# Sink-window attention with a two-layer MLP on one core: start-up order, three engine moves and the last output step

## The chip, the cores and the metric

One core of a Trainium2 chip runs the kernel. Its engines work side by side and meet at semaphores: TensorE (PE, with the weight loads shown apart as PEld), VectorE (DVE), ScalarE (ACT), GpSimd (POOL), and SyncE (SP), whose queue issues nearly all DMAs. Each engine works through its own list in order. The metric is device time in microseconds (us), as the median of three runs.

## The reference

Batch 4, 8 heads, 768 positions, head size 64, float32. Query i sees keys of a window, `0 <= i - k < window` (128 here), and the first `n_sink` keys (4 here):

```python
keep = is_sink | in_window
scores = np.where(keep, scale * q @ k.T, -1e9)
a = exp(scores - max); a = a / (sum(a) + 1e-9)
x = (a @ v)                       # heads side by side: 3072 tokens x 512
h = x @ w_in                      # 512 x 2048
g = np.maximum(0.01 * h, h)
out = g @ w_out                   # 2048 x 512
```

`n_sink` and `window` come as data, so the masks are computed on the chip.

## The kernel before, in words

The work is cut into 8 units (a batch's first or second 384 tokens), named u. A unit has an attention part, four head pairs, and an MLP part, 16 steps over the hidden dimension (fc). A unit's MLP needs x of its four pairs.

**Start.** `body` makes `ident` (for transposes on PE) and calls `build_masks`. That loads the two limits by DMA and writes masks m0, m1, m2 (for the first, second and later query tiles), and also what only units 2 to 7 use: `tri`, `low`, `upp` and the packed masks `pm`. GpSimd writes rel, key, low, upp, and copies m1 to m2 (line 89) after DVE has made m1. Only behind that copy, in `fast_path`, GpSimd zeroes `wz` (line 211), the operand of WARM = 16 small bf16 matmuls that open PE's list (line 216), and the sink buffers `sk` (line 220).

**Attention of units 0 and 1** ("native", both heads of a pair at once). For each query tile j: the scores on PE (line 240), max with the mask on DVE (line 252), exp on ACT (line 254), a copy of the four sink columns to `sk` on GpSimd (line 388). Then, some tile steps later (LAGT, LAGG, LAGV), PE transposes the weights (line 279) and ACT copies them to `pt` (line 283); `gather` transposes the sink weights and the reciprocal sums (lines 305, 309), which ACT and DVE copy out (lines 313, 316, 317); `values` multiplies with v (line 326) and with the sink values sv (line 333). DVE scales the result (line 339), ACT rounds it to xh (line 340) and GpSimd makes the remainder xl (line 341). The sink values arrive by DMA as svr; ACT rounds them to sv (line 194), GpSimd subtracts (line 195).

**Weights.** Each of 16 w_in and 16 w_out tiles arrives as 64-bit words and is decoded by three DVE instructions (lines 141, 143, 145), rounded by ACT (line 149), and its remainder made by GpSimd (line 150). The first is told to stand behind an attention instruction on DVE (`tc.issue_after`). Three fc are loaded during unit 0's attention, the others in unit 0's MLP.

**MLP.** Step fc puts 12 matmuls h (line 465: four x tiles, three terms each) on PE; ACT, DVE, ACT, GpSimd make g, gh and gl from it (lines 472 to 475, 2.7 us in a row); then PE runs the o matmuls of the step before it: gh with both halves of w_out for each of three token tiles (line 487), then gl for the three (line 492). With fc = 15 the three tiles are copied out by DVE (line 503; the very last tile in halves, ACT at line 498 and DVE at line 500) and written by SP.

**Order.** PE's list is written out by hand: `attention_stream` and `mlp_stream` are generators. 32 + LEAD0 steps of attention go first (32 are unit 0's), then attention steps are taken between MLP steps at due times that rise from LEAD0 to LEAD = 12 steps ahead. The lists of the other engines and of SP are made by the framework's planner from the program's order and its own time model. Pools of buffers set when a tile may be written: tag io has three buffers (svr, decoded weights, outputs), tag raw three, tag qksp (the q and k of a pair, qkn) two.

Of the kernel before, what the change touches and what calls it, by code (L numbers as in the profile page):

```python
# [12 lines left out]
I8 = mybir.dt.int8  # L13
# [27 lines left out]
LEAD = 12  # L41
LEAD0 = 5
LAGT = 2
# [5 lines left out]
PRED = 3  # L49
WARM = 16  # L50
W_LO = 1.125 * 2.0 ** -15
# [4 lines left out]
def build_masks(nc, cpool, tpool, lims):  # L56
# [31 lines left out]
    nc.vector.tensor_scalar(out=m1, in0=m1, scalar1=-1.0, scalar2=MASKED, op0=ALU.add, op1=ALU.mult)  # L88
    nc.gpsimd.tensor_copy(out=m2, in_=m1)
    nc.vector.tensor_scalar(out=m2[:, snk], in0=key[:, 0:NSK], scalar1=ns, scalar2=-1.0, op0=ALU.is_lt,  # L90
                            op1=ALU.add)
    nc.vector.tensor_scalar(out=m2[:, snk], in0=m2[:, snk], scalar1=MASKED, scalar2=None, op0=ALU.mult)
    tri = cpool.tile([P, P], I8, name="tri")
    low = cpool.tile([P, P], F32, name="low")
    upp = cpool.tile([P, P], F32, name="upp")
    nc.vector.tensor_scalar(out=tri, in0=rel[:, P:], scalar1=0.0, scalar2=None, op0=ALU.is_lt)
    nc.gpsimd.memset(low, 1.0)
    nc.gpsimd.affine_select(out=upp, in_=low, pattern=[[1, P]], base=0, channel_multiplier=-1,
                            compare_op=ALU.is_ge, fill=0.0)
    nc.gpsimd.affine_select(out=low, in_=low, pattern=[[-1, P]], base=-1, channel_multiplier=1,  # L100
                            compare_op=ALU.is_ge, fill=0.0)
    pm = [m0]
    for i, m in enumerate((m1, m2)):
# [3 lines left out]
        pm.append(pk)  # L107
    return lim, (m0, m1, m2), pm, tri, low, upp


@with_exitstack
def fast_path(ctx, tc, cpool, qp, qk, vu, vs, wq, out, ident, lim, masks, pmasks, tri, low, upp, negm, wmin,
              wmax):
    nc = tc.nc
# [13 lines left out]
    raws, vraws, svs = {}, {}, {}  # L128
    sks = []

# [59 lines left out]
    def load_sinks(u, pair):  # L190
        raw = iopool.tile([SKR, TU], F32, tag="io", name=f"svr{u}_{pair}", bufs=3)
        nc.sync.dma_start(out=raw, in_=vs[u // 2, pair])
        sv = apool.tile([SKR, TU], F32R, tag="sv", name=f"sv{u}_{pair}")
        nc.scalar.copy(out=sv, in_=raw)
        (nc.gpsimd if native(u) else nc.vector).tensor_tensor(out=sv[D:96, :], in0=raw[D:96, :],
                                                              in1=sv[D:96, :].bitcast(F32), op=ALU.subtract)
        svs[u, pair] = sv
# [11 lines left out]

    wz = wpool.tile([P, 2 * P], mybir.dt.bfloat16, name="wz")  # L210
    nc.gpsimd.memset(wz, 0.0)
    warm = bank("h", "warm")
# [72 lines left out]
    def turn_packed(u, pair, o, w, state):  # L285
# [12 lines left out]
        n = T - 1 + half  # L298
        for t, mask in enumerate((low, upp)):
            nc.vector.tensor_tensor(out=dst[:, t], in0=src,  # L300
                                    in1=mask.rearrange("p (o q) -> p o q", o=1).broadcast_to([P, n, P]), op=ALU.mult)
# [18 lines left out]
    def values(u, pair, state):  # L320
# [16 lines left out]
        if native(u):  # L337
            xf = state["r"]
            nc.vector.tensor_tensor(out=xf, in0=acc[:, 0:TU], in1=xf, op=ALU.mult)
            nc.scalar.copy(out=xh, in_=xf)  # L340
            nc.gpsimd.tensor_tensor(out=xl, in0=xf, in1=xh.bitcast(F32), op=ALU.subtract)  # L341
        else:
            nc.scalar.copy(out=xh, in_=acc[:, 0:TU])
            nc.vector.tensor_tensor(out=xl, in0=acc[:, 0:TU], in1=xh.bitcast(F32), op=ALU.subtract)
# [7 lines left out]
    def attend(u, pair, pend):  # L352
# [3 lines left out]
        def later(lag, f):  # L356
            pend.append((count[0] + lag, f))
# [19 lines left out]
        if native(u):  # L377
            state["sm"] = apool.tile([P, T, 2], F32, tag="sm", name=f"sm{u}_{pair}")
            sp = raws.pop((u, pair))
            for j in range(T):  # L380
# [10 lines left out]
                if j == 0:  # L391
                    fetch(0)
                    load_sinks(u, pair)
                count[0] += 1
                if j == T - 1:
# [3 lines left out]
        else:  # L399
            for o in range(2):  # L400
# [8 lines left out]
                for j in range(T):  # L409
                    ps, = scores(u, pair, j, (o,), sp)  # L410
                    if KSL[u % 2][j][1] == W3:
                        nc.vector.copy_predicated(out=ps[:, W1:W3], mask=tri, data=ps[:, 0:P])
                        src = ps[:, P:W3]
                    else:
                        src = ps[:, 0:W1]
                    soft(u, h, j, w[:, j], src, pmasks[min(T * (u % 2) + j, 2)], sm[:, j:j + 1])
                    count[0] += 1
# [9 lines left out]
                    yield  # L427
        later(LAGG, lambda: gather(u, pair, state))
        later(LAGV, lambda: values(u, pair, state))

# [18 lines left out]
    def mlp_stream():  # L449
        po = {}  # L450
        prev = None
        for step in range(NU * NFC + 1):
# [26 lines left out]
            if prev is not None:  # L479
                v, f, gh, gl = prev  # L480
                if f == 0:
                    po = [bank(f"o{t}", f"o{v}_{t}") for t in range(T)]
                wh, wl = wts["o", f]
                for t in range(T):
                    tsl = slice(t * P, (t + 1) * P)
                    for c, w in enumerate((wh, wl)):
                        nc.tensor.matmul(po[t], lhsT=gh[:, tsl], rhs=w, start=f == 0 and c == 0, stop=False)  # L487
                    if t < T - 1:
                        yield v
                for t in range(T):  # L490
                    tsl = slice(t * P, (t + 1) * P)
                    nc.tensor.matmul(po[t], lhsT=gl[:, tsl], rhs=wh, start=False, stop=f == NFC - 1)  # L492
                    if f == NFC - 1:
                        last = v == NU - 1 and t == T - 1
                        ob = iopool.tile([P, 512], F32, tag="raw" if last else "io", name=f"ob{v}_{t}", bufs=3)
                        r0 = (v * T + t) * P
                        if last:
                            nc.scalar.copy(out=ob[:, 0:256], in_=po[t][:, 0:256])
                            nc.scalar.dma_start(out=out[r0:r0 + P, 0:256], in_=ob[:, 0:256])
                            nc.vector.tensor_copy(out=ob[:, 256:], in_=po[t][:, 256:])  # L500
                            nc.sync.dma_start(out=out[r0:r0 + P, 256:], in_=ob[:, 256:])
                        else:
                            nc.vector.tensor_copy(out=ob, in_=po[t])
                            nc.sync.dma_start(out=out[r0:r0 + P, :], in_=ob)
                yield v
# [164 lines left out]
def body(tc, qp0, qp1, qk0, qk1, vu0, vu1, vs, wq, qT, kT, v, lims, w_in, w_out, out):  # L670
# [3 lines left out]
    wq = wq.bitcast(I32)  # L674
    with tc.tile_pool(name="cpool", bufs=1) as cpool:
        ident = cpool.tile([P, P], F32, name="ident")
        make_identity(nc, ident)
# [3 lines left out]
        with tc.tile_pool(name="tpool", bufs=1) as tpool:  # L681
            lim, masks, pmasks, tri, low, upp = build_masks(nc, cpool, tpool, lims)
        flag = fast_path(tc, cpool, (qp0, qp1), (qk0, qk1), (vu0, vu1), vs, wq, out, ident, lim, masks,
                         pmasks, tri, low, upp, negm, wmin, wmax)
        bad = nc.values_load(flag[0:1, 0:1], min_val=0, max_val=1)
# [49 lines left out]
```

## Time and profile before

| what | us |
|---|---|
| median of 3 runs | 722.77 (722.31 to 724.15) |
| the profiled execution: its own time | 722.46 |
| its span, first to last instruction | 720.7 |
| busy: PE, DVE, POOL, ACT | 689.8, 430.1, 371.4, 346.9 |

A row of the timeline gives the start, the duration, the engine, line and operation, the tile written and those read, and in brackets the idle time of the engine before it with what ended it. A row of windows gives busy time by engine in a stretch, then PE's granted clock as a share of 2.4 GHz, the DMA share and rate.

### The profile page before, as it was taken

To read this page: it belongs to the slowest core of one execution; us is meant where nothing else is said; L and a number is where in the kernel's file an instruction comes from. 1 tells how busy PE (TensorE), PEld (TensorE's weight loads), DVE (VectorE), ACT (ScalarE), POOL (GpSimd) and SP (SyncE) were. 2 spreads that over 40 slices of the span, in tenths; PEclk is the share of its full clock that TensorE was granted. 3 is DMA by queue.
4 is the path that set the end of the run, shared out by engine and by line. 5 is a ranking of instruction groups with operands and counts; after the bars stand their busy time and mean duration, and the time that the engine had idled before them with its cause. 6 is when DMAs were issued, how large, how long until landed. Compare 5 with 4: busy or idle time off the path is not lost.

```text
span 720.7 us, 11518 instructions
## 1 busy us (share of the span) xinstructions
PE 689.8 (96%) x3917; PEld 594.5 (82%) x3917; DVE 430.1 (60%) x1190; ACT 346.9 (48%) x938; POOL 371.4 (52%) x424
## 2 busy tenths in 40 slices
PE   6879989999999999999999999999999999999995
PEld 3448778888888888887898888888888888799894
DVE  5866989765557576665667676675566755411111
ACT  4765575554444555445555454545554444222221
POOL 4666677644354665655665565556556443122220
PEclk9899999999999999999999999999999999999998
DMA  6656566341222533253332534334342400001001
GB/s 215 219 168 194 180 205 216 123 147 38 67 70 88 170 107 120 80 157 131 121 108 82 181 106 126 114 99 158 108 135 80 132 16 1 1 0 45 1 1 49
DMA packets 30307, 78.51 MB, mean 109 GB/s; under 512 B 3488, under 2 KB 9888, under 8 KB 30240
## 3 DMA queue, kind: packets, MB, share of 16 engines
q1 hardware_dynamic: 30096, 77.56, 33.8%
q8 instruction: 33, 0.54, 0.3%
q14 instruction: 34, 0.28, 0.1%
q10 hardware_dynamic: 144, 0.13, 0.1%
HBM read 71.39 MB, written 6.29 MB: 108 GB/s over the span
## 4 chain that ended last, share of the span: by engine, by line
PE 83%; DVE 6%; ACT 3%; DMA 3%; issue 2%; POOL 2%; DVEq 0%; POOLq 0%; ACTq 0%; SPq 0%
PE h L465 33%; PE o L487 23%; PE o L492 11%; PE acc L326 5%; PE s L245 4%; DMA svr<-in_vs 2%; PE t L289 2%; ACT pk L254 2%; PE acc L333 2%; PE s L240 1%; PE t L279 1%; POOL zero L160 1%; DVE g L473 1%; PE warm L216 1%; DVE pk L421 1%
## 5 line engine op out<-in xcount | busy, mean ns | idle before, releaser
L475 POOL TENSOR_TENSOR gl<-g,gh 128x384 fp32r<-128x384 f32 x127 | 138.9, 1094 | 200.4 <-ACT gh L474 197.4
L465 PE MATMUL h<-xh,wih 128*128 128x384 f32 x512 | 180.3, 352 | 2.0 <-DVE g L473 2.0
L465 PE MATMUL h<-xl,wih 128*128 128x384 f32 x512 | 172.4, 337 | 0.7 <-POOL xl L341 0.7
L465 PE MATMUL h<-xh,wil 128*128 128x384 f32 x512 | 172.6, 337 | 0.0
L487 PE MATMUL o<-woh,gh 128*128 128x512 f32 x384 | 155.8, 406 | 2.9 <-ACT gh L474 2.9
L487 PE MATMUL o<-wol,gh 128*128 128x512 f32 x384 | 151.7, 395 | 0.0
L473 DVE TENSOR_TENSOR g<-h,g 128x384 f32<-128x384 f32 x128 | 71.3, 557 | 111.9 <-ACT g L472 110.4
L474 ACT CAST gh<-g 128x384 fp32r<-128x384 f32 x128 | 65.5, 512 | 93.7 <-DVE g L473 92.5
L492 PE MATMUL o<-woh,gl 128*128 128x512 f32 x384 | 109.8, 394 | 0.0
L465 PEld LDWEIGHTS h<-xh,wih 128*128 128x128 f32 x512 | 96.5, 188 | 10.7 <-DVE g L473 2.4
L254 ACT ACTIVATE pk<-pk,negm 128x132 f32<-128x132 f32 (+1 forms) x192 | 81.4, 424 | 44.6 <-DVE negm L252 43.4
L465 PEld LDWEIGHTS h<-xl,wih 128*128 128x128 f32 x512 | 96.7, 189 | 5.8 <-POOL xl L341 1.1
L472 ACT ACTIVATE g<-h 128x384 f32<-128x384 f32 x128 | 62.4, 487 | 74.8 <-PE h L465 74.2
L465 PEld LDWEIGHTS h<-xh,wil 128*128 128x128 f32 x512 | 96.2, 188 | 0.0
L492 PEld LDWEIGHTS o<-woh,gl 128*128 128x128 f32 x384 | 72.2, 188 | 17.1
L204 POOL TENSOR_TENSOR qksp<-qkraw,qksp 64x396 fp32r<-64x396 f32 (+1 forms) x48 | 56.6, 1178 | 57.6 <-issue 51.7
L487 PEld LDWEIGHTS o<-woh,gh 128*128 128x128 f32 x384 | 72.7, 189 | 11.7 <-ACT gh L474 4.2
L487 PEld LDWEIGHTS o<-wol,gh 128*128 128x128 f32 x384 | 72.6, 189 | 7.0
L245 PEld LDWEIGHTS s<-qksp 128*128 128x128 f32 x288 | 53.2, 188 | 6.4
L203 ACT CAST qksp<-qkraw 128x780 fp32r<-128x780 f32 (+1 forms) x48 | 42.9, 894 | 28.4 <-PE s L245 26.8
L245 PE MATMUL s<-qksp 128*128 128x260 f32 (+1 forms) x288 | 56.1, 276 | 0.0
L160 POOL TENSOR_SCALAR zero<-mag 128x512 f32<-128x512 f32 x32 | 48.0, 1500 | 15.7 <-ACT mag L159 9.1
(109 smaller groups left out, 911.7 us busy)
## 6 DMA issues: line engine op xcount, KB each, us to landing
craw<-in_wq SPq DMA_DIRECT2D x32, 512.0 KB, 3.9
qkraw<-in_qk SPq DMA_DIRECT2D x24, 454.0 KB, 3.2
qkraw<-in_qk SPq DMA_DIRECT2D x24, 390.0 KB, 3.0
wiraw<-in_wq SPq DMA_DIRECT2D x16, 512.0 KB, 3.9
woraw<-in_wq SPq DMA_DIRECT2D x16, 512.0 KB, 3.6
svr<-in_vs SPq DMA_DIRECT2D x32, 192.0 KB, 2.8
out<-ob SPq DMA_DIRECT2D x23, 256.0 KB, 2.6
v<-in_vu SPq DMA_DIRECT2D x16, 256.0 KB, 3.0
```

Of the source, the lines that this page charges most:

```text
L160: nc.gpsimd.tensor_scalar(out=zero, in0=mag, scalar1=0.0, scalar2=None, op0=ALU.is_equal)
L203: nc.scalar.copy(out=sp[:, 0:TU + n], in_=raw[:, 0:TU + n])
L204: nc.gpsimd.tensor_tensor(out=sp[D:P, TU:TU + n], in0=raw[D:P, TU:TU + n], in1=sp[D:P, TU:TU + n].bitcast(F32), op=ALU.subtract)
L245: nc.tensor.matmul(pss[0][:, 0:kn], lhsT=sp[:, off + j * P:off + (j + 1) * P], rhs=sp[:, TU + k0:TU + k0 + kn], start=c == 0, stop=c == 1)
L254: nc.scalar.activation(out=w, in_=w, func=AF.Exp, scale=-1.0, bias=neg, accum_out=sm)
L465: nc.tensor.matmul(ph[:, 0:TU], lhsT=w[:, cs], rhs=x, start=cc == 0 and c == 0, stop=cc == NCC - 1 and c == 2)
L472: nc.scalar.mul(g, ph[:, 0:TU], 0.01)
L473: anchor[0] = nc.vector.tensor_tensor(out=g, in0=ph[:, 0:TU], in1=g, op=ALU.max)
L474: nc.scalar.copy(out=gh, in_=g)
L475: (nc.vector if step == NU * NFC - 1 else nc.gpsimd).tensor_tensor(out=gl, in0=g, in1=gh.bitcast(F32), op=ALU.subtract)
L487: nc.tensor.matmul(po[t], lhsT=gh[:, tsl], rhs=w, start=f == 0 and c == 0, stop=False)
L492: nc.tensor.matmul(po[t], lhsT=gl[:, tsl], rhs=wh, start=False, stop=f == NFC - 1)
```

## The change

- The zeros `wz` move to `body`, ahead of `ident`: they are GpSimd's first work of the kernel. WARM goes from 16 to 17.
- `build_masks` keeps m0, m1 and m2; m2's copy from m1 becomes two copies without the sink columns. `late_masks` writes low, upp, tri and pm, and is called in unit 0's third pair, behind its sink load. tri, a DVE compare before, becomes a GpSimd select and a copy; the select uses a buffer of tag io.
- In unit 0 the rounding of svr to sv goes from ACT to GpSimd, and so does that of x to xh for pairs 0 to 2.
- The last pair of unit 0 gathers and sums after LAGT = 2 tile steps in place of 3 and 4, and LEAD0 goes from 5 to 3, so PE's list has two steps of unit 1's attention fewer ahead of the first h.
- The o matmuls are one list. Up to fc = 14 their order is as before, with the places at which attention steps may come in moved to behind each third. With fc = 15 they run tile by tile (gh, gh, gl), and each tile is copied out as its third matmul is placed.

```diff
-LEAD0 = 5
+LEAD0 = 3
-WARM = 16
+WARM = 17
...
-    nc.gpsimd.tensor_copy(out=m2, in_=m1)
+    nc.gpsimd.tensor_copy(out=m2[:, prv], in_=m1[:, prv])
+    nc.gpsimd.tensor_copy(out=m2[:, cur], in_=m1[:, cur])
...
+def late_masks(nc, cpool, tpool, masks):
+    m0, m1, m2 = masks
...
-    nc.vector.tensor_scalar(out=tri, in0=rel[:, P:], scalar1=0.0, scalar2=None, op0=ALU.is_lt)
     nc.gpsimd.memset(low, 1.0)
     nc.gpsimd.affine_select(out=upp, in_=low, pattern=[[1, P]], base=0, channel_multiplier=-1,
                             compare_op=ALU.is_ge, fill=0.0)
+    sel = tpool.tile([P, P], F32, tag="io", name="sel", bufs=3)
+    nc.gpsimd.affine_select(out=sel, in_=low, pattern=[[1, P]], base=-1, channel_multiplier=-1,
+                            compare_op=ALU.is_ge, fill=0.0)
     nc.gpsimd.affine_select(out=low, in_=low, pattern=[[-1, P]], base=-1, channel_multiplier=1,
                             compare_op=ALU.is_ge, fill=0.0)
+    nc.gpsimd.tensor_copy(out=tri, in_=sel)
     pm = [m0]
     for i, m in enumerate((m1, m2)):
         nc.gpsimd.tensor_copy(out=pk[:, 0:NSK], in_=m[:, snk])
         nc.vector.tensor_tensor(out=pk[:, NSK:], in0=m[:, prv], in1=m[:, cur], op=ALU.max)
...
-        nc.scalar.copy(out=sv, in_=raw)
+        (nc.scalar.copy if u else nc.gpsimd.tensor_copy)(out=sv, in_=raw)
...
-    wz = wpool.tile([P, 2 * P], mybir.dt.bfloat16, name="wz")
-    nc.gpsimd.memset(wz, 0.0)
...
-            nc.scalar.copy(out=xh, in_=xf)
+            (nc.gpsimd.tensor_copy if u == 0 and pair < NPAIR - 1 else nc.scalar.copy)(out=xh, in_=xf)
...
                     load_sinks(u, pair)
+                    if u == 0 and pair == 2:
+                        late.append(late_masks(nc, cpool, iopool, masks))
...
-        later(LAGG, lambda: gather(u, pair, state))
-        later(LAGV, lambda: values(u, pair, state))
+        last = u == 0 and pair == NPAIR - 1
+        later(LAGT if last else LAGG, lambda: gather(u, pair, state))
+        later(LAGT if last else LAGV, lambda: values(u, pair, state))
...
-                for t in range(T):
+                order = [(t, c) for t in range(T) for c in range(2)] + [(t, 2) for t in range(T)]
+                if f == NFC - 1:
+                    order.sort()
+                for i, (t, c) in enumerate(order):
                     tsl = slice(t * P, (t + 1) * P)
-                    for c, w in enumerate((wh, wl)):
-                        nc.tensor.matmul(po[t], lhsT=gh[:, tsl], rhs=w, start=f == 0 and c == 0, stop=False)
-                    if t < T - 1:
+                    nc.tensor.matmul(po[t], lhsT=(gl if c == 2 else gh)[:, tsl], rhs=wl if c == 1 else wh,
+                                     start=f == 0 and c == 0, stop=f == NFC - 1 and c == 2)
+                    if i in (2, 5):
                         yield v
-                for t in range(T):
-                    tsl = slice(t * P, (t + 1) * P)
-                    nc.tensor.matmul(po[t], lhsT=gl[:, tsl], rhs=wh, start=False, stop=f == NFC - 1)
-                    if f == NFC - 1:
+                    if f < NFC - 1 or c < 2:
+                        continue
...
+        wz = cpool.tile([P, 2 * P], mybir.dt.bfloat16, name="wz")
+        nc.gpsimd.memset(wz, 0.0)
         ident = cpool.tile([P, P], F32, name="ident")
```

## Rows read from the trace of the kernel before

**Rows 1.** The page's first part: busy time, share of the span, instructions.
```profile
PE 689.8 (96%) x3917; PEld 594.5 (82%) x3917; DVE 430.1 (60%) x1190; ACT 346.9 (48%) x938; POOL 371.4 (52%) x424
```
**Rows 2.** Windows: the first unit's attention, two parts of it, its MLP.
```profile
10.54:46.80 36.26, 29.28 (x194) 17.62 (x193) 26.29 (x96) 28.28 (x93) 20.65 (x47) 0.91 0.58 195
20.20:27.90 7.70, 7.43 (x33) 4.35 (x33) 6.16 (x19) 4.84 (x15) 4.52 (x8) 0.56 0.54 178
27.90:37.70 9.80, 7.39 (x57) 4.33 (x55) 8.05 (x26) 8.74 (x28) 7.30 (x15) 1.00 0.77 260
46.80:135.00 88.20, 83.54 (x480) 68.80 (x478) 74.23 (x162) 54.88 (x133) 66.16 (x77) 0.98 0.61 192
```
**Rows 3.** Timeline of the start: a mask, the zeros, warm-up, scores, first weight decode.
```profile
5.42 0.22 DVE L84 TENSOR_SCALAR m<-m 128x132 f32<-128x132 f32 x1
...
6.76 0.31 POOL L211 MEMSET wz<- 128x256 bf16 x1 [0.20 <-DVE m L90]
...
7.13 3.48 PE L216 MATMUL warm<-wz 128*128 128x256 bf16 x16 [7.13 <-POOL wz L211]
...
10.54 1.80 PE L240 MATMUL s<-qkn 64*128 64x132 f32 x12
11.06 0.30 DVE L252 CUSTOM_DVE_ANT_0 pk<-s,m 128x132 f32<-128x132 f32 x1 [3.97 <-PE s L240]
...
13.82 0.69 DVE L141 TENSOR_SCALAR di<-wiraw 128x512 int32<-128x512 int32 x1
```
**Rows 4.** SP's queue: the first load of q and k, the first weight load.
```profile
1.25 0.42 SPq L174 DMA_DIRECT2D qkn<-in_qp  x1
...
4.10 0.43 SPq L136 DMA_DIRECT2D wiraw<-in_wq  x1
```
**Rows 5.** From issue to landing, us: that load of qkn, then that wiraw.
```profile
DMA to landing us min/median/max: 3.8/3.8/3.8
...
DMA to landing us min/median/max: 5.6/5.6/5.6
```
**Rows 6.** Groups by line up to 46.8 us: casts, copies and selects that move.
```profile
L194 ACT CAST sv<-svr 128x384 fp32r<-128x384 f32 x6 | 3.1, 511 | 8.9 <-DMA svr<-in_vs 8.5 <-PE acc L333 0.4
...
L266 POOL COPY rb<-sm 128x384 f32<-128x384 f32 x5 | 2.5, 505 | 1.4 <-DVE sm L264 1.4
...
L98 POOL TENSOR_SCALAR_AFFINE_SELECT upp<-low 128x128 f32<-128x128 f32 x1 | 0.3, 288 | 0.0
```
**Rows 7.** Timeline of ACT: a sink rounding that waited for its DMA.
```profile
40.54 0.51 ACT L194 CAST sv<-svr 128x384 fp32r<-128x384 f32 x1 [2.03 <-DMA svr<-in_vs]
```
**Rows 8.** Timeline: one DVE instruction twice, the second beside a GpSimd one.
```profile
14.57 0.17 DVE L263 TENSOR_SCALAR sm<-sm 128x6 f32<-128x6 f32 x1
...
29.81 1.27 POOL L150 TENSOR_TENSOR wol<-wo,woh 128x512 fp32r<-128x512 f32 x1 [0.33 <-PE t L279]
...
30.10 1.00 DVE L263 TENSOR_SCALAR sm<-sm 128x6 f32<-128x6 f32 x1
```
**Rows 9.** Timeline of PE: the same four transposes in two stretches.
```profile
23.95 1.11 PE L279 MATMUL t<-ident,pk 128*128 128x128 f32 x4
...
31.57 0.66 PE L279 MATMUL t<-ident,pk 128*128 128x128 f32 x4
```
**Rows 10.** Timeline of the end: the last gl, o, copies and output DMA.
```profile
710.39 0.56 DVE L475 TENSOR_TENSOR gl<-g,gh 128x384 fp32r<-128x384 f32 x1 [0.58 <-ACT gh L474]
...
710.56 0.40 PE L487 MATMUL o<-woh,gh 128*128 128x512 f32 x1
...
711.96 0.86 PE L492 MATMUL o<-woh,gl 128*128 128x512 f32 x3
712.40 1.29 DVE L503 COPY ob<-o 128x512 f32<-128x512 f32 x2 [1.45 <-PE o L492]
...
713.60 0.41 DVE L500 COPY ob<-o 128x256 f32<-128x256 f32 x1
...
714.28 0.41 SPq L501 DMA_DIRECT2D out<-ob  x1
```

More of the change, by code (lines that the diff above doesn't have):

```diff
@@ L92, in build_masks @@
     nc.vector.tensor_scalar(out=m2[:, snk], in0=m2[:, snk], scalar1=MASKED, scalar2=None, op0=ALU.mult)
-    tri = cpool.tile([P, P], I8, name="tri")
+    return lim, (m0, m1, m2)
+def late_masks(nc, cpool, tpool, masks):
+    m0, m1, m2 = masks
+    prv, snk, cur = slice(0, P), slice(P, W1), slice(W1, W3)
     low = cpool.tile([P, P], F32, name="low")
     upp = cpool.tile([P, P], F32, name="upp")
-    nc.vector.tensor_scalar(out=tri, in0=rel[:, P:], scalar1=0.0, scalar2=None, op0=ALU.is_lt)
+    tri = cpool.tile([P, P], I8, name="tri")
     nc.gpsimd.memset(low, 1.0)
@@ L107, in build_masks, with fast_path @@
         pm.append(pk)
-    return lim, (m0, m1, m2), pm, tri, low, upp
+    return pm, tri, low, upp
 @with_exitstack
-def fast_path(ctx, tc, cpool, qp, qk, vu, vs, wq, out, ident, lim, masks, pmasks, tri, low, upp, negm, wmin,
-              wmax):
+def fast_path(ctx, tc, cpool, qp, qk, vu, vs, wq, out, ident, lim, masks, wz, negm, wmin, wmax):
     nc = tc.nc
@@ L128, in fast_path @@
     raws, vraws, svs = {}, {}, {}
-    sks = []
+    sks, late = [], []
     def load_weights(fc):
@@ L298, in turn_packed @@
         n = T - 1 + half
-        for t, mask in enumerate((low, upp)):
+        for t, mask in enumerate(late[0][2:]):
             nc.vector.tensor_tensor(out=dst[:, t], in0=src,
@@ L411, in attend @@
                     if KSL[u % 2][j][1] == W3:
-                        nc.vector.copy_predicated(out=ps[:, W1:W3], mask=tri, data=ps[:, 0:P])
+                        nc.vector.copy_predicated(out=ps[:, W1:W3], mask=late[0][1], data=ps[:, 0:P])
                         src = ps[:, P:W3]
@@ L415, in attend @@
                         src = ps[:, 0:W1]
-                    soft(u, h, j, w[:, j], src, pmasks[min(T * (u % 2) + j, 2)], sm[:, j:j + 1])
+                    soft(u, h, j, w[:, j], src, late[0][0][min(T * (u % 2) + j, 2)], sm[:, j:j + 1])
                     count[0] += 1
@@ L489, in mlp_stream @@
                         yield v
-                for t in range(T):
-                    tsl = slice(t * P, (t + 1) * P)
-                    nc.tensor.matmul(po[t], lhsT=gl[:, tsl], rhs=wh, start=False, stop=f == NFC - 1)
-                    if f == NFC - 1:
[L494 to L504, printed above, removed]
+                    if f < NFC - 1 or c < 2:
+                        continue
@@ new lines, in mlp_stream @@
+                    last = v == NU - 1 and t == T - 1
+                    ob = iopool.tile([P, 512], F32, tag="raw" if last else "io", name=f"ob{v}_{t}", bufs=3)
+                    r0 = (v * T + t) * P
+                    if last:
+                        nc.scalar.copy(out=ob[:, 0:256], in_=po[t][:, 0:256])
+                        nc.scalar.dma_start(out=out[r0:r0 + P, 0:256], in_=ob[:, 0:256])
+                        nc.vector.tensor_copy(out=ob[:, 256:], in_=po[t][:, 256:])
+                        nc.sync.dma_start(out=out[r0:r0 + P, 256:], in_=ob[:, 256:])
+                    else:
+                        nc.vector.tensor_copy(out=ob, in_=po[t])
+                        nc.sync.dma_start(out=out[r0:r0 + P, :], in_=ob)
@@ L681, in body @@
         with tc.tile_pool(name="tpool", bufs=1) as tpool:
-            lim, masks, pmasks, tri, low, upp = build_masks(nc, cpool, tpool, lims)
+            lim, masks = build_masks(nc, cpool, tpool, lims)
         flag = fast_path(tc, cpool, (qp0, qp1), (qk0, qk1), (vu0, vu1), vs, wq, out, ident, lim, masks,
-                         pmasks, tri, low, upp, negm, wmin, wmax)
+                         wz, negm, wmin, wmax)
         bad = nc.values_load(flag[0:1, 0:1], min_val=0, max_val=1)
```

## The prediction
> **What bounds the kernel now.** I read the page's first part, then windows, then the timeline of the stretches in which PE isn't full. PE is busy 96% of the span [rows 1], so a gain can come from two places: PE's idle time, and PE's time at a low clock. The windows show where that is [rows 2]. Unit 0's attention, from the first score at 10.54 to the first h at 46.8, is 36.3 us with PE busy 29.3; its MLP, to 135, is 88.2 us with PE busy 83.5. What comes later is PE's own work, and no engine move of the change reaches it. In the attention stretch no engine is full: ACT is busy 28.3 of 36.3, DVE 26.3, GpSimd 20.7. It is a chain of short steps through four engines, in which whoever is late holds PE, whose list is in fixed order.
>
> Ahead of it stand 10.54 us without a score. The timeline tells why [rows 3]: the zeros are written at 6.76, behind the last mask on DVE, so the 16 warm-up matmuls run from 7.13 to 10.61 and the first score follows at once. The scores' data came much earlier: the load issued at 1.25 [rows 4] landed 3.8 us later [rows 5], at 5.05. The mask of the first tile was done at 5.64 [rows 3]. So the zeros alone kept PE's list shut.
>
> **The change, part by part.**
>
> *Zeros first, 17 warm-ups.* GpSimd can write the zeros at the place of its first memset, before 1.2 us. I put PE's start there. At 3.48 / 16 = 0.217 us each [rows 3], 17 take 3.7 us, so they end at about 4.9, where the data lands at 5.05. First score near 5.1, that is 5.4 us earlier. The first mask step needs m0, done at 5.64, so it can stand near 5.7 in place of 11.06: also 5.4 less. The first weight decode limits this. It stands at 13.82 [rows 3], after seven mask steps and before the rest of pair 1's, and DVE can't pass it. Its DMA was issued at 4.10 [rows 4] and landed 5.6 us later [rows 5], at 9.7. These loads don't move: they wait for no engine. If DVE's list keeps its order, the decode starts at 9.7, so the stream behind it moves up by 13.82 − 9.7 = 4.1. If the planner puts mask steps ahead of it, up to 5.4. If the later masks (m2's two copies are on GpSimd now and follow m1) are put ahead of the first mask step, that one stands near 7 and the gain at that place is 4, much the same. Lower end 3, for a first mask step at 7 with its chain then late at the decode as well. I take **4.1**: it is the end that a row fixes.
>
> *Late masks.* They take from the start one GpSimd memset and two selects, which had waited for nothing there, and add to the middle of unit 0 five GpSimd instructions of 128x128 (0.29 each by the select's row [rows 6], so 1.4 us) with two tiny copies, and on DVE two max instructions, which leave the start. tri's select holds an io buffer for a moment; SP's next sink load or the next weight may wait for it, and with the planner free to move them I price it with the next item.
>
> *sv and xh on GpSimd.* A rounding of 128x384 costs ACT 0.511; GpSimd's copy of the same shape, from another source, costs 0.505 [rows 6]. Seven go over in unit 0: ACT loses 3.6 us, GpSimd gains 3.5. In the middle (27.9 to 37.7) ACT is busy 8.74 of 9.80 and GpSimd 7.30 [rows 2]. Four of the seven can fall there: ACT goes to 6.7. GpSimd gets 2.0, and 1.4 of masks: 10.7 for 9.8. So the chain is freed at one engine and filled at the other. Best end: what ACT sheds is all on the path, +2.0. Worst end: the 3.4 us stand ahead of a sink copy or a reciprocal that PE waits for, −3.4. I take **0**, between the two. ACT's wait of 2.03 at 40.54 [rows 7] stays: that sink load is unit 1's first, and unit 1's rounding stays on ACT. In the sum it goes nowhere; if it goes away as the lists shift, +2.0 more.
>
> *LAGT for the last pair, LEAD0 3.* PE's list has gather and values of the last pair one step after the other, and h two attention steps earlier. PE's work is the same, so only idle time can go. PE is idle 36.3 − 29.3 = 7.0 us in the attention stretch and 88.2 − 83.5 = 4.7 in the MLP [rows 2]; the two steps that move touch only the end of the one and the start of the other. Against a gain: values now follows gather with no score between them, and x of the last pair is made in a chain that h waits for; and unit 0's MLP takes 41 attention steps in place of 39, while DVE is busy there 74.2 of 88.2 [rows 2]. Bounds +1.5 and −1.5. I take **+0.4**, near zero, since the chain from gather to xl is as long as before.
>
> *The last o step.* At the end PE runs six o matmuls from 710.56 and three from 711.96 (0.233 each), then DVE copies two whole tiles from 712.40 and half of the last at 713.60, and SP issues that half's DMA at 714.28 [rows 10]. Tile by tile, the first tile's gl is wanted at 710.56 + 2 × 0.233 = 711.02; DVE has written it at 710.95, so no wait. The first tile is complete near 711.4, the second near 712.1, each copied (0.65) before the next; the last is complete at 712.82 as before, and its half is copied from 712.9 to 713.3. The DMA goes out near 713.35 in place of 714.28, behind less traffic: **+1.0** (bounds 0.6 and 1.8). At the seven other unit ends nine o matmuls (2.1 us at 0.233) and twelve h matmuls lie between a step's h and its o, so gl is there in time; 0. The places at which attention may come in move by a matmul or two: 0, and with it ±0.5.
>
> *Sum.* 4.1 + 0 + 0.4 + 1.0 = 5.5 us. Against the profiled execution's own 722.46 (1.8 more than its span, which I leave as it is) that is 717.0. The median is 0.3 above it, so **717.3**.
>
> **A cost that the sum leaves out, by row and by rule.** DVE's small step on the sums took 0.17 us once and 1.00 while GpSimd subtracted [rows 8]. The Trainium skill, "SBUF — State Buffer", section "SBUF: two separate sides", says that DVE and GpSimd share a pair of ports under a lock, held for a whole instruction, so that one blocks fully. The rows agree: the long one ends when the subtraction does. By that rule each of the seven moved roundings could hold a DVE step, up to 3.5 us in all, a sum of 2.0 in place of 5.5.
>
> **Rivals.**
>
> *A, more than the sum.* The window 20.2 to 27.9 has a mean granted clock of 0.56 (1.00 is 2.4 GHz), with PE busy 7.43 of 7.70 [rows 2]. At 2.4 GHz that work is 7.43 × 0.56 = 4.2, so 3.3 us go if the stretch doesn't come back. With ACT's 2.0 from [rows 7] the gain is up to 10.8. For it: ACT is the engine with the least to spare in the attention stretch, and it sheds work. Against: four of its seven roundings may come only after that window. Time 711.5 to 715.
>
> *B, GpSimd becomes the bound.* The 3.4 us of the middle are all late, ahead of the copies that gather needs, or the lock above takes as much from DVE: 5.5 − 3.4 = 2.1, so **720.6**. For it: GpSimd's 10.7 of 9.8. Against: sink roundings and masks can be done early or in gaps; over the whole stretch GpSimd has 15 us free.
>
> *C, the change doesn't do what it says.* The planner places the first mask step behind work that waits, or a DMA that the shifted stream asks for lands late, and what the start gives is idle time again before the first h. Only the tail is left: about **721.8**. Against: the rows show data and mask at 5.05 and 5.64.
>
> *D, slower.* One mechanism: the clock. The warm-up now runs while the loads are still under way, and the first scores then wait for masks; if PE has the low level through unit 0's attention, its work there is longer. The same four transposes take 1.11 at the low level and 0.66 at the high one [rows 9], ratio 1.68. PE's busy time outside the low window is 29.3 − 7.4 = 21.9; × 0.68 = 14.9 more, less what idle time takes up (36.3 − 29.3 = 7.0): 7.9, so **725.2**. It decides once over 5.5 of these 7.9 us come, so two thirds of the attention at the low level. Against: in the kernel before 16 warm-ups were enough; in the window behind the low one the clock is 1.00 under the same kind of work [rows 2].
>
> **How the numbers follow.** The sum (715 to 719.6): 0.56. A: 0.17. B (719.6 to 721): 0.14. C: 0.06. D: 0.07. The likeliest is 717.3. The range 713.0 to 721.0 takes in most of A and all of B; under 0.2 is left out, on A's far end, C and D. A measurement of this kernel tells a change from none at about 0.3%, 2.2 us: below 720.6 is faster. All of the first two, and about 0.10 of B: 0.83. C and the rest of B: 0.10. D: 0.07.
>
> **What would show it.** Right: warm-up from near 1.2 to 4.9, first score near 5.1, first mask step between 5.7 and 7, first decode near 9.7 with DVE idle ahead of it, first h near 41, the last output DMA issued 0.9 us sooner after the last matmul. GpSimd's busy time up to the first h should rise by some 5 us and ACT's fall by 3.6. Wrong: a first h later than 44 (B, C or D, told apart by who PE waits for and by the granted clock), or PE idle in unit 0's MLP well over 4.7 us, which would mean that what the start gave is taken back there.

## The result, and the profile after

The changed kernel takes 715.99 us (715.04 to 717.52, 4 runs) against 722.54 (721.5 to 724.15, 4 runs): ratio 0.9909 [0.9884, 0.9935], so 6.5 us sooner. The profiled execution of it is the slowest of its four, 717.52; its span is 715.8, against 720.7, so the traces explain 4.9 of the 6.5.

The first part of the page (compare [rows 1]): PE does the same work. Of the moves one sees ACT fall and GpSimd rise.
```profile
PE 689.6 (96%) x3918; PEld 594.5 (83%) x3918; DVE 423.8 (59%) x1189; ACT 344.9 (48%) x931; POOL 377.0 (53%) x434
```

The timeline of the start (compare [rows 3]):
```profile
0.80 0.31 POOL L688 MEMSET wz<- 128x256 bf16 x1 [0.29 <-POOLq L738]
...
1.17 3.81 PE L223 MATMUL warm<-wz 128*128 128x256 bf16 x17 [1.17 <-POOL wz L688]
...
5.13 0.93 PE L247 MATMUL s<-qkn 64*128 64x132 f32 x8
...
5.71 0.22 DVE L84 TENSOR_SCALAR m<-m 128x132 f32<-128x132 f32 x1
...
6.38 0.29 DVE L259 CUSTOM_DVE_ANT_0 pk<-s,m 128x132 f32<-128x132 f32 x1
...
9.74 0.69 DVE L150 TENSOR_SCALAR di<-wiraw 128x512 int32<-128x512 int32 x1 [0.53 <-DMA wiraw<-in_wq]
```
The first score stands 5.41 us sooner (5.13 for 10.54), the first mask step 4.68, the first decode 4.08 (9.74 for 13.82), and DVE is idle for 0.53 ahead of it, for the weight's DMA. Up to here the trace is what the prediction wrote down. But the first h starts at 45.05. The mark set for it was near 41, and 4.1 sooner alone would be 42.7.

Windows of the kernel after (compare [rows 2]): first score to first h, unit 0's MLP up to the first h of unit 1's, and from there to the first h of the very last step ("the last h" below). The prediction's window of unit 0's MLP ended at 135.00; unit 1's first h is at 142.73, and PE's idle time up to there is the same 4.7 us.
```profile
5.13:45.05 39.92, 29.44 (x184) 17.89 (x185) 26.82 (x101) 25.40 (x83) 27.19 (x62) 0.87 0.64 217
45.05:139.14 94.09, 91.12 (x527) 75.04 (x526) 79.90 (x181) 60.14 (x148) 70.30 (x84) 1.00 0.60 191
139.14:701.79 562.65, 558.67 (x3165) 493.93 (x3164) 312.69 (x895) 256.72 (x696) 276.76 (x278) 1.00 0.28 89
```
The last two of these stretches in the kernel before:
```profile
46.79:142.73 95.94, 91.28 (x521) 75.65 (x519) 79.27 (x176) 59.32 (x145) 70.12 (x82) 0.98 0.58 181
142.73:706.39 563.66, 559.41 (x3165) 493.75 (x3164) 318.39 (x894) 255.66 (x695) 274.44 (x278) 1.00 0.28 89
```
This is the account of the 4.9 us. Start: 5.41 gained. Unit 0's attention: 39.92 in place of 36.25, 3.67 given back; PE is busy about as long (29.44, 29.27), so it is idle for 10.5 us where it was for 7.0. Unit 0's MLP: 1.85 gained. The rest up to the last h: 1.01. From the last h to the end: 14.28 became 14.03, 0.25. In this execution most of what the start gave is gone again by the first h, and stretches from which the sum took little or nothing gained.

### The profile page after: what moved, and what is told of

Read it like the earlier page. It is cut to its first block, busy times and chain, and to the rows that moved or that the text cites. A ratio compares the mean times of both kernels' runs of the same rounds, so it can differ in the third digit from the quotient of the medians.

```text
span 715.8 us, 11514 instructions
## 1 busy us (share of the span) xinstructions
PE 689.6 (96%) x3918; PEld 594.5 (83%) x3918; DVE 423.8 (59%) x1189; ACT 344.9 (48%) x931; POOL 377.0 (53%) x434
## 4 chain that ended last, share of the span: by engine, by line
PE 87%; DMA 4%; DVE 3%; ACT 2%; POOL 2%; issue 1%; SPq 1%; ACTq 0%; POOLq 0%; DVEq 0%
PE h L475 35%; PE o L499 35%; PE acc L333 5%; PE s L252 4%; PE t L296 2%; DMA svr<-in_vs 2%; PE acc L340 2%; PE s L247 1%; PE t L286 1%; DMA craw<-in_wq 1%; DMA wiraw<-in_wq 1%; PE sk L312 0%; DMA out<-ob 0%; DVE wi L154 0%; DVE di L150 0%
## 5 line engine op out<-in xcount | busy, mean ns | idle before, releaser
L485 POOL TENSOR_TENSOR gl<-g,gh 128x384 fp32r<-128x384 f32 x127 | 141.1, 1111 | 204.9 <-ACT gh L484 204.7
L499 PE MATMUL o<-woh,gh 128*128 128x512 f32 x384 | 151.5, 395 | 2.5 <-ACT gh L484 2.5
L499 PE MATMUL o<-woh,gl 128*128 128x512 f32 x384 | 113.7, 398 | 0.0
L213 POOL TENSOR_TENSOR qksp<-qkraw,qksp 64x396 fp32r<-64x396 f32 (+1 forms) x48 | 56.7, 1180 | 57.3 <-issue 46.9
L499 PEld LDWEIGHTS o<-woh,gl 128*128 128x128 f32 x384 | 69.3, 188 | 13.5 <-DVE gl L485 0.2
```

The lines of the kernel that those rows point to most:

```text
L213: nc.gpsimd.tensor_tensor(out=sp[D:P, TU:TU + n], in0=raw[D:P, TU:TU + n], in1=sp[D:P, TU:TU + n].bitcast(F32), op=ALU.subtract)
L485: (nc.vector if step == NU * NFC - 1 else nc.gpsimd).tensor_tensor(out=gl, in0=g, in1=gh.bitcast(F32), op=ALU.subtract)
L499: nc.tensor.matmul(po[t], lhsT=(gl if c == 2 else gh)[:, tsl], rhs=wl if c == 1 else wh, start=f == 0 and c == 0, stop=f == NFC - 1 and c ...
```

## Experiments

All are timed in 5 rounds beside runs of the kernel before (721.9, 721.6 and 722.7 us in the three groups). Where two ratios are subtracted below, the half-widths of their intervals are put together as the root of their squares. "First h" is the start of the first h matmul in the profiled execution, 46.79 before and 45.05 after. The four parts that can be undone are the moves to GpSimd, LEAD0 with LAGT, the o order, and the masks.

**start_only**: the kernel before, with the zeros first and 17 warm-ups, nothing else.
```
-WARM = 16
+WARM = 17
...
-    wz = wpool.tile(...)          # in fast_path, behind build_masks
-    nc.gpsimd.memset(wz, 0.0)
...
+        wz = cpool.tile(...)      # ahead of build_masks
+        nc.gpsimd.memset(wz, 0.0)
```


> The kernel before with the zeros written first and 17 warm-ups, nothing else. Theory 1 (the start pays, and pays to the end): first score at 5.1 as in the changed kernel, first weight decode at 9.7, and the whole stream 4 us earlier at the first h (42.5 to 43) and at the end: 717.5 to 719. Rival (the start is taken back inside unit 0's attention, and the changed kernel's gain is from its other parts): first h at 45 or later, 720.5 to 722.5.


719.15 us, 0.9949 [0.9926, 0.9971]: 3.7 us sooner (2.1 to 5.4). The first h is at 42.83, 3.96 sooner, unit 1's MLP starts 3.71 sooner, the last h 3.12. So the start alone brings to the first h what the decode's DMA allows, and by the times nearly all of it lasts. The one trace is less even: at the second h step PE waits 1.5 us for g and has the low level from 47.53 to 50.95, so at the third step the lead is 2.0 us (54.83 for 56.78), and it is back at 3.7 behind the place where the kernel before has its own low stretch (92.28 to 95.69). What the whole change lost before the first h, another part of it took.

**moves_back**: the kernel after, with both roundings on ACT.
```
-        (nc.scalar.copy if u else nc.gpsimd.tensor_copy)(out=sv, in_=raw)
+        nc.scalar.copy(out=sv, in_=raw)
...
-            (nc.gpsimd.tensor_copy if u == 0 and pair < NPAIR - 1 else nc.scalar.copy)(out=xh, in_=xf)
+            nc.scalar.copy(out=xh, in_=xf)
```


> The changed kernel with the roundings to sv and xh on ScalarE again. Theory 1 (the moves cost: in the trace of the changed kernel ScalarE's copy r waits up to 1.3 us for GpSimd's xl, which has one buffer r and now comes later): these waits go, first h at 42 to 44 in place of 45.05, time 713.5 to 715.5. Rival (the moves relieve ScalarE and are worth what it shed): first h at 46 to 48, time 717 to 719.


711.22 us, 0.9853 [0.9827, 0.988]. This is the lowest median of all the runs, below the range expected for it; the moves cost 0.0056 of the time, 4.0 us (±2.6). First h 41.97. What PE waited for between first score and first h, in the kernel after (columns: total, times, longest):
```profile
PE acc L340 <- DVE st L324: 5.7, 3, 2.0
PE t L286 <- DVE r L346: 2.6, 3, 1.9
PE sk L316 <- POOL rb L273: 1.2, 1, 1.2
```
and in moves_back:
```profile
PE t L286 <- DVE r L346: 3.2, 3, 1.7
PE acc L340 <- DVE st L324: 1.9, 2, 1.2
PE sk L316 <- POOL rb L273: 1.2, 1, 1.2
```
One row is longer by much, the matmul of the sinks' values, which waits for st: 3.8 us more. Shorter rows go the other way, so in all PE is idle for 10.5 us of this stretch after and for 8.1 in moves_back; it is also busy 0.6 longer, with 10.2 us at the low level (18.66 to 25.49, 39.14 to 42.55) against 6.8. The timeline of one such place shows why. After:
```profile
33.15 0.33 PE L312 MATMUL sk<-ident,sk 128*128 128x128 f32 x1
...
34.78 0.51 POOL L203 CAST sv<-svr 128x384 fp32r<-128x384 f32 x1 [1.42 <-DMA svr<-in_vs]
...
35.10 0.21 DVE L270 TENSOR_SCALAR sm<-sm 128x6 f32<-128x6 f32 x1 [0.96 <-ACT pk L261]
...
35.38 0.99 POOL L348 TENSOR_TENSOR xl<-r,xh 128x384 fp32r<-128x384 f32 x1
...
36.41 0.48 ACT L320 COPY r<-sk 128x384 f32<-128x384 f32 x1 [1.34 <-POOL xl L348]
...
37.09 0.28 DVE L324 TENSOR_TENSOR st<-sk,st 32x128 fp32r<-32x128 f32 x1 [1.55 <-ACT st L323]
...
37.43 0.44 PE L340 MATMUL acc<-st,sv 128*128 128x128 f32 x2 [1.75 <-DVE st L324]
```
The same place in moves_back:
```profile
32.84 0.33 PE L312 MATMUL sk<-ident,sk 128*128 128x128 f32 x1
...
34.04 0.46 ACT L320 COPY r<-sk 128x384 f32<-128x384 f32 x1
...
34.70 0.28 DVE L324 TENSOR_TENSOR st<-sk,st 32x128 fp32r<-32x128 f32 x1 [0.85 <-ACT st L323]
...
35.30 0.44 PE L340 MATMUL acc<-st,sv 128*128 128x128 f32 x2
```
From gather to that matmul it is 2.46 us with the roundings on ACT and 4.28 on GpSimd. Read the chain backwards: PE waits for st, DVE waits for ACT, ACT waits to overwrite r until GpSimd's xl has read it, and xl stands behind a rounding that waits 1.42 for the *next* sink load. On GpSimd the wait for a sink load held xl, and through it three engines. In moves_back ACT waits for no sink load before the first h.

**sv_back** and **xh_back**: the kernel after with one rounding each on ACT, the first and the second half of the diff above.


> The changed kernel with only the rounding of the sink values on ScalarE again (xh stays on GpSimd). Theory 1a (the harm is GpSimd's queue standing behind svr's DMA with xl and the sink copies behind it: 2.3 and 1.4 us of wait at 23.5 and 34.8 in the changed kernel): most of the 5 us that both moves cost comes back, 711 to 713.5, first h at 42 to 43. Rival 1b (the harm is xh before xl on one engine): 714.5 to 717, first h at 44 to 45.5.

> The changed kernel with only xh on ScalarE again (sv stays on GpSimd). Theory 1a (the harm is GpSimd waiting for svr's DMA): little comes back, 714.5 to 717, first h at 44 to 45.5. Rival 1b (the harm is xh before xl on one engine, which holds r longer): 711 to 713.5, first h at 42 to 43.


sv_back: 711.85 us, 0.9871 [0.9852, 0.989], 2.7 us (±2.3) below the kernel after. xh_back: 714.71, 0.9913 [0.9896, 0.9931], the same as after. So the sinks' rounding, which waits for a DMA, carries most of the price, and x's rounding, which waits for DVE, little that these times can tell from none. In the profiled execution of sv_back GpSimd waits for no sink load; in that of xh_back it still does:
```profile
POOL sv L203 <- DMA svr<-in_vs: 2.1, 1, 2.1
```
xh_back's own first h was early, though (41.22). PE then waits 3.1 us for g at the second h step and has the low level from 48.40 to 51.81, and its third h step starts at 54.15. There the executions stand in the order of the times: 51.03 in moves_back, 51.05 in sv_back, 54.09 in the kernel after, 54.15 in xh_back. The row of PE that waits for st doesn't rank them (it was 3.9 before). sv_back:
```profile
PE acc L340 <- DVE st L324: 3.3, 2, 2.6
```
xh_back:
```profile
PE acc L340 <- DVE st L324: 2.4, 2, 2.0
```
So the chain above is shown for one place of the kernel after, and the price of the sinks' rounding by times; that the whole price runs through this chain is not shown. A second reading is open beside it. The mean granted clock of the executions went along with the times: 0.9900 in the four of the kernel after and 0.9902 in xh_back's, 0.9932 in sv_back's and 0.9937 in moves_back's. By these means up to 2.6 us of the 4.0 (0.0037 of 715, an estimate) could be time at the low level. In the kernel after and in moves_back each fall to it in unit 0 comes behind a wait of PE of 1.1 to 1.9 us, so the waits may bring it on; but the same kind of wait (1.98 us, up to 91.55 in lead5 below) is followed by no fall, and no run separates the two.

**r2**: the kernel after with two buffers for r, so that ACT's copy needn't wait for xl.
```
-            r = xpool.tile([P, TU], F32, tag="r", name=f"r{u}_{pair}", bufs=1)
+            r = xpool.tile([P, TU], F32, tag="r", name=f"r{u}_{pair}", bufs=2)
```


> The changed kernel with two buffers for r in place of one, so that the next pair's copy of r doesn't wait for xl. Theory 1c (the one buffer of r carries GpSimd's lateness to ScalarE, 1.3 us once and 0.2 once, and so to st and PE): these two waits go, 0.5 to 2 us faster than the changed kernel, 713.5 to 715.5. Rival (ScalarE only waits elsewhere, for DVE or PE, in the same place): 715.5 to 717.


715.64 us, 0.9927 [0.991, 0.9943], as after. ACT waits for xl no longer, but the row of PE is still there:
```profile
PE acc L340 <- DVE st L324: 3.5, 2, 2.0
```
and so is GpSimd's wait for sink loads (3.4 us in three waits). The buffer was how one of the waits reached PE, not what caused it. Here, too, the first h of the profiled execution is early (42.14); PE then waits 2.4 us for g at the second step, and the third starts at 52.88, sooner than in the kernel after, which the time doesn't show.

**lead5**: the kernel after with the old LEAD0 and lags.
```
-LEAD0 = 3
+LEAD0 = 5
...
-        last = u == 0 and pair == NPAIR - 1
-        later(LAGT if last else LAGG, lambda: gather(u, pair, state))
-        later(LAGT if last else LAGV, lambda: values(u, pair, state))
+        later(LAGG, lambda: gather(u, pair, state))
+        later(LAGV, lambda: values(u, pair, state))
```


> The changed kernel with LEAD0 = 5 and the old delays for the last pair. Theory 1 (the start pays, this part is worth little): 716 to 717, PE idle in unit 0's MLP up to 16 steps within 1 us of the changed kernel's 3. Rival (this part is what removed the stalls of unit 0's MLP, 1.9 us and a low clock near step 7 and 1.3 us at step 13 in the kernel before): the stalls come back, 718.5 to 720.5.


717.78 us, 0.9951 [0.9934, 0.9969], between the two ranges expected: without this part 3.0 us (±2.2) of the gain are gone. **mb_lead5**, the same edit on moves_back:


> The changed kernel with sv and xh on ScalarE and with LEAD0 = 5 and the old delays for the last pair. Against the kernel with the moves alone taken back (0.985 of before): theory 3 (LEAD0 and the delays remove the stalls of about 3 us near steps 7 and 13 of unit 0's MLP, whatever the moves): the stalls are back and it is 2 to 4 us slower, 0.988 to 0.991 of before. Rival (part of the first difference was the state of the clock and the planner's later lists): within 1 us of it, 0.984 to 0.987.


715.79 us, 0.9892 [0.9859, 0.9924], against 0.9853: 2.8 us (±3.0). It is about the same size on two bases, though the second interval just reaches zero. The trace shows it in unit 0's MLP, where PE is idle for 3.0 us in the kernel after and for 4.7 in lead5. What PE waits for there, 46 to 143 us, before:
```profile
PE h L465 <- DVE g L473: 2.0, 2, 1.3
PE t L279 <- ACT pt L283: 1.9, 1, 1.9
PE h L465 <- POOL xl L341: 0.7, 1, 0.7
```
and after:
```profile
PE acc L333 <- issue: 1.6, 1, 1.6
PE h L475 <- DVE g L483: 1.1, 2, 0.7
PE t L286 <- ACT pt L290: 0.2, 1, 0.2
```
The row with "issue" is new. In mb_lead5 the first two rows of before are back:
```profile
PE h L474 <- DVE g L482: 2.8, 2, 1.5
PE t L286 <- ACT pt L290: 1.9, 1, 1.9
```
With LEAD0 = 5 transposes of unit 1's attention, placed between two h steps, wait 1.8 to 2.0 us for pt in all four kernels that have it (before, start_only, lead5, mb_lead5), and 0.2 in the ten with 3. The lags aren't in this: they concern unit 0's last pair, whose x the first h step already needs. In the kernel before it looks like this:
```profile
90.30 0.84 ACT L203 CAST qksp<-qkraw 128x780 fp32r<-128x780 f32 x1 [0.70 <-DMA qkraw<-in_qk]
...
91.05 0.61 ACT L149 CAST wih<-wi 128x512 fp32r<-128x512 f32 x1
...
91.57 0.58 ACT L283 COPY pt<-t 128x512 f32<-128x512 f32 x1
...
92.20 1.08 PE L279 MATMUL t<-ident,pk 128*128 128x128 f32 x4 [1.91 <-ACT pt L283]
```
ACT's copy to pt stands behind a rounding that waits for a load, here the q and k of a later unit: the same pattern as on GpSimd above. PE then has the low level, 1.2 GHz:
```profile
92.28:95.69 3.41, 3.41 (x11) 3.08 (x12) 2.33 (x5) 3.01 (x9) 3.33 (x6) 0.50 0.92 296
```
3.41 us of busy PE at 0.50, so up to another 1.7 lost. mb_lead5 has such a stretch at 90.1, too; lead5 and start_only have the stall without it. So the stall is shown wherever LEAD0 is 5, the low clock behind it in two kernels of four.

**o_old**: the kernel after with the old order of the last o step and the old places at which attention comes in.
```
-                if f == NFC - 1:
-                    order.sort()
...
-                    if i in (2, 5):
+                    if i in (1, 3):
```


> The changed kernel with the o matmuls in the old order and the old places for attention steps. Theory 1 (worth the tail's 0.4 us and no more): 716 to 717, last DMA issued 0.4 us later after the last matmul. Rival (the even places for attention steps remove stalls in the MLP as well): 717.5 to 719.


718.38 us, 0.9953 [0.9932, 0.9973], so this part is worth 3.2 us (±2.4). **mb_oold**, the same edit on moves_back:


> The changed kernel with sv and xh on ScalarE and the o matmuls in the old order. Theory 4 (worth the tail's 0.4 us and at most 1 us at unit ends): 0.985 to 0.987 of before. Rival (the new places for attention steps carry 2 us or more, as the first look at the old order suggested): 0.988 to 0.990.


715.53 us, 0.9904 [0.9873, 0.9935], against 0.9853: 3.7 us (±2.9). From the last matmul's end to the end of the span it is 8.11 us with the old order (mb_oold) and 7.29 with the new one (moves_back), so the tail is 0.8 of it; from o_old to the kernel after it is 0.1 (7.61, 7.47). The rest should lie ahead of it, from the first h of unit 1's MLP to the last h. In mb_oold:
```profile
135.88:699.06 563.18, 559.51 (x3165) 493.82 (x3164) 318.76 (x894) 255.83 (x695) 275.28 (x278) 1.00 0.28 89
```
in moves_back:
```profile
135.38:695.86 560.48, 558.59 (x3165) 493.94 (x3164) 312.31 (x895) 257.13 (x696) 277.83 (x278) 1.00 0.28 90
```
2.7 us: PE's busy time is 0.9 less and its idle time 1.8 less (3.67 and 1.89). This pair is the far end: from o_old (563.15) to the kernel after (562.65) the same stretch gains only 0.5, and those two profiled executions, 717.07 and 717.52, don't show the 3.2 us at all. Over all kernels the order is plain. The four with the old order, before, start_only, o_old and mb_oold, take 563.2 to 564.3 us for this stretch; the ten with the new one take 560.5 to 562.7: 1.8 less on the mean, and PE is busy for 559.4 to 559.5 against 558.6 to 559.0. The tail is 0.7 less on the mean. The waits in the stretch, mb_oold first:
```profile
PE o L497 <- ACT gh L484: 2.3, 4, 1.2
PE t L296 <- DVE deep L553: 1.4, 1, 1.4
```
and moves_back:
```profile
PE t L296 <- DVE deep L555: 0.9, 1, 0.9
PE o L499 <- ACT gh L484: 0.9, 1, 0.9
```
Some steps' o wait for gh, in both. How often isn't settled by the order alone: the kernel after has the new order and 2.5 us of these waits, and its stretch is 562.65. It differs from moves_back by 2.2 us there, though the two moves touch unit 0 only; the planner orders the other engines' lists anew for each kernel, and what that does to later units is in every time here.

**masks_early**: moves_back with all masks built at the start, as before.
```
-    nc.gpsimd.tensor_copy(out=m2[:, prv], in_=m1[:, prv])
-    nc.gpsimd.tensor_copy(out=m2[:, cur], in_=m1[:, cur])
+    nc.gpsimd.tensor_copy(out=m2, in_=m1)
...
-    return lim, (m0, m1, m2)
...
-def late_masks(nc, cpool, tpool, masks):
...
+    nc.vector.tensor_scalar(out=tri, in0=rel[:, P:], scalar1=0.0, scalar2=None, op0=ALU.is_lt)
```


> The kernel with sv and xh on ScalarE, zeros first, LEAD0 3 and delays, new o order, but all masks built at the start as in the kernel before. Theory 5 (the late masks are worth nothing: the planner puts two of the three selects and the packed masks at the start anyway): 0.984 to 0.987 of before, first mask step within 0.5 us of 6.4. Rival (they clear the start): first mask step 0.7 us later or more, 0.987 to 0.990.


712.79 us, 0.986 [0.9835, 0.9885], against 0.9853: no difference. In the kernel after, a memset and a select of the late part still run at 1.77 and 2.25, and DVE's two max at 6.17 and 7.16, among the first mask steps; only the rest came later.

**spread** and **spread5**: moves_back with weights fetched at every eighth and fifth attention step in place of every third (`PRED = 3` to 8 and 5).


> The changed kernel with sv and xh on ScalarE and the three early weight loads spread over unit 0's attention (PRED 8 in place of 3: steps 11, 19, 27 in place of 6, 9, 12). Theory 2 (with the earlier start DVE's weight decodes are what holds the first two pairs, DVE busy 9.5 of 9.7 us there, the first decode even waits for its DMA): the first pairs go faster, first h at 39.5 to 41.5, time 708.5 to 711. Rival (DVE's work only moves, and the third weights are late for the MLP): first h or the first MLP steps later by as much, 711 to 713.5.

> The changed kernel with sv and xh on ScalarE and the early weight loads at steps 8, 13 and 18 (PRED 5), between the tight ones (6, 9, 12) and the spread ones (11, 19, 27), of which the latter had the first h 4 us sooner and gave 2.3 back at the second h. Theory 2: part of the sooner first h stays and nothing is given back, 0.981 to 0.984 of before. Rival (what decides is when DVE has all weights of the first steps): 0.984 to 0.988.


spread: 712.09 us, 0.9873 [0.9851, 0.9895]; spread5: 711.88, 0.985 [0.9818, 0.9883]; both as moves_back. In spread5 the first h stays (41.75). In spread it comes at 38.04, 3.9 us sooner than in moves_back, but PE then waits within the first two steps, for x's remainder and for g:
```profile
PE h L475 <- DVE g L483: 1.5, 1, 1.5
PE h L475 <- POOL xl L348: 0.7, 1, 0.7
```
and has the low clock from 43.5 to 46.9. By the third h step the lead over the kernel before is 6.5 us, down from 8.7. So an early first h is worth only what the steps behind it can keep up, as in xh_back, r2 and start_only.

## Why the prediction was right in sum and wrong in three of its terms

The forecast was 717.3, faster; the time is 715.99. It wasn't right for its reasons alone: the moves came 4.0 us worse than the sum had them, the other two terms 4.8 to 5.1 better, and that these nearly cancel is luck. Term by term (measured as above):

| term | predicted, us | measured, us |
|---|---|---|
| start | 4.1 | 3.7 (start_only) |
| sv, xh to GpSimd | 0 (−3.4 to 2.0) | −4.0 (moves_back) |
| LAGT, LEAD0 | 0.4 (±1.5) | 3.0, 2.8 (lead5, mb_lead5) |
| last o step, its places | 1.0 (0.6 to 1.8), 0 ± 0.5 | 3.2, 3.7 (o_old, mb_oold) |
| late masks | within the moves | 0 (masks_early) |
| sum | 5.5 | 5.9, or 6.2 by the second of each; the change: 6.5 |

- **Start: right, with its limit.** Score, mask step and decode stand where they were put, and the limit was the weight's DMA. Rival D, the low level through two thirds of the attention, didn't come: from 5.13 to 9.74 the granted clock is 1.00, the 2.4 GHz level, in the kernel after. A milder form of it is there: 10.2 us of the attention stretch are at the low level, where it was 6.8 before.
- **Moves: wrong size, and rival B's case.** The step that failed is the 0 "between the two" ends. It weighed busy time, 10.7 for 9.8 in a window, and kept the queue for the worst end and for B; what it cost, 4.0 (±2.6), lies at that worst end. The prediction had itself seen ACT's 2.03 wait for a sink load [rows 7]; here a rounding that waits like this took its wait along to the engine it was moved to. Placed on GpSimd it waited 3.8 us in two waits before the first h, with xl and copies behind it. The note that a first h after 44 means B, C or D holds: it came at 45.05, at the place shown PE waited through ACT and DVE for GpSimd, and by that note it is B, in mechanism and not in time. GpSimd's busy time up to the first h rose by 3.2 (25.92 to 29.08), ACT's fell by 3.9 (30.57 to 26.68).
- **The port lock was not the price.** DVE's small step on the sums took 0.21 at 35.10, beside the rounding of 34.78, where [rows 8] had 0.17 alone and 1.00 beside a subtraction, and DVE's busy time up to the first h is 28.34 in the kernel after and 28.91 in moves_back, for 109 instructions in both. By the rule of the Trainium skill, "SBUF — State Buffer", section "SBUF: two separate sides", that step should have been held, as in [rows 8], until the rounding ended, at 35.29; it ended at 35.31, so the place allows either, and at most 0.04 us hangs on it.
- **LAGT, LEAD0: mis-sized, 2.9 for 0.4.** The prediction saw PE's idle 4.7 us in the MLP and didn't ask which waits made it. Two rows would have told: the 1.9 for pt and the 2.0 for g. The step that failed is "the two steps that move touch only the end of the one and the start of the other": the due time of every attention step in unit 0's MLP starts from LEAD0, so the edit shifts them all, and the stall for pt, far from either end (92.20), goes from 1.9 to 0.2. It also said that "x of the last pair is made in a chain that h waits for" and counted this against a gain; with both edits, and two steps fewer ahead of it, the first h came 1.1 us sooner (lead5 to after) and 0.8 (mb_lead5 to moves_back).
- **Last o step: mis-sized.** Of the 1.0 for the tail 0.1 to 0.8 came, by the pair compared (0.4 from before to after). Two things took the rest, both to be seen in the tail of the kernel after (compare [rows 10]):
```profile
706.45 0.19 PEld L499 LDWEIGHTS o<-woh,gl 128*128 128x128 f32 x1 [0.25 <-DVE gl L485]
...
706.98 1.39 DVE L514 COPY ob<-o 128x512 f32<-128x512 f32 x2 [0.59 <-PE o L499]
...
708.38 0.37 ACT L509 COPY ob<-o 128x256 f32<-128x256 f32 x1 [2.58 <-PE o L499]
708.79 0.42 DVE L511 COPY ob<-o 128x256 f32<-128x256 f32 x1 [0.41 <-ACT ob L509]
709.46 0.39 SPq L512 DMA_DIRECT2D out<-ob  x1
```
DVE's half of the last tile waits 0.41 for ACT's half of the same tile, and from that half's end to its DMA it is 0.25 us, where the sum had 0.05 though [rows 10] show 0.27. So the DMA goes out 1.11 us after the last matmul's end, not 0.5; before it was 1.46. The "no wait" for gl was nearly right: the weight load of gl comes 0.25 late, since gl is written from 705.83 to 706.39, but the nine matmuls take 2.34 us in place of 2.26. The larger share came where the prediction had "0, and with it ±0.5": seven other unit ends and the places of attention, by the times 2 to 3 us and by the traces 1.8 on the mean, between unit 1 and the last h.
- **Rival A**, 711.5 to 715, didn't come for this kernel, and its way is not what brought moves_back to 711.2. The low stretch of the attention didn't go: after has 0.50 from 18.66 to 25.49 and from 39.14 to 42.55. What went is the one in the MLP.

Open: how much of the price of the moves is waits and how much the low level; how the 2 to 3 us of the o order split between the order at unit ends and the places of attention, which were changed together only; why PE is busy 0.5 to 0.9 us less there; and how far the parts act on each other: sv_back and xh_back give 2.7 and 0 of the 4.0 of moves_back, which their scatter allows but doesn't settle.

## What to carry to other kernels

Before a step is moved to an engine with time to spare, look up what the step waits for: its wait goes with it, and holds what is queued behind it there; leave a step that waits for a load on the engine where the least hangs behind it. When a window shows idle time on the engine that bounds the kernel, list the waits that make it up before pricing an edit that shifts steps in that window. And a forecast that is right in sum may hide errors that cancel: undo each part by itself, and the kernel with the lowest median here, 711.2 us at 0.9853 [0.9827, 0.988], is the change without the part that cost.

## What the runs showed of the hardware that wasn't expected

- PE falls to the low level in unit 0 in every kernel, but at other places and for other totals: 20.60 to 27.43 and 92.28 to 95.69 before, 18.66 to 25.49 and 39.14 to 42.55 after, 18.74 to 22.15 and 28.98 to 32.4 in moves_back. At 0.50, each 3.4 us cost up to 1.7. Single executions of one kernel lie up to 5 us apart, and the clock goes along: moves_back's fastest, 708.64, had a mean granted clock of 0.998, its slowest, 714.01, 0.991.
- GpSimd rounds 128x384 in 0.51 us, ACT in 0.51: the moved work cost what it had cost, only the waits were new.
